# A decode block that streams its cache: other buffers for the last head's values, wo and w2

## The chip, the core and the metric

The kernel runs on one core of one Trainium2 chip. The metric is the device time of one execution in microseconds, as the median of several runs. The profile shows one execution, and its own time is given beside its span.

## What is computed

One token passes through an attention block with a key and value cache and a gated feed-forward block. A sigmoid gate mixes the two results. All data are float32.

```python
# x (1,1,512), k_cache and v_cache (1,8,32768,128), wq (512,4096), wo (4096,512), w1, w3 (512,1792), w2 (1792,512)
g = _sigmoid((x * gate_w).sum(-1, keepdims=True))
q = (x @ wq).reshape(B, Sq, 32, 128).transpose(0, 2, 1, 3)
k, v = jnp.repeat(k_cache, 4, axis=1), jnp.repeat(v_cache, 4, axis=1)
p = _softmax(jnp.einsum("bhqd,bhkd->bhqk", q, k) * (128 ** -0.5), axis=-1)
a = jnp.einsum("bhqk,bhkd->bhqd", p, v).transpose(0, 2, 1, 3).reshape(B, Sq, 4096) @ wo
b = (_silu(x @ w1) * (x @ w3)) @ w2
return g * a + (1 - g) * b
```

## The kernel before

There are 8 key and value heads, each serving 4 query heads. The keys of one head are 16.8 MB and so are its values. They are loaded in two halves of 8.39 MB. On chip there are three regions of that size, 128 partitions by 16384 floats each: `ra` takes the first half of a head's keys, `rb` the second half, and `rc` one half of its values at a time. At the start `rc` holds wq, and `rb` holds w1 and w3.

All large loads are issued by SyncE (SP) on one DMA queue, in an order that is written out by hand, with a semaphore wait ahead of each load whose region must first come free. Two counters tell when that is so:

- `c_k` counts the scores products: `2*h + 1` means that the first half of head h's keys (in `ra`) has been used, `2*h + 2` that the second half (in `rb`) has been.
- `c_v` counts the values products in the same way: `2*h + 1` after the first half of head h's values, `2*h + 2` after the second.

VectorE (DVE) turns the keys in place in their region, in blocks of 32 by 32 (`turned`), and signals each piece with `t_tr`. TensorE (PE) runs a loop over the heads. A step makes the scores of the first half (`scores(0, ra)`), the sum of the previous head's probabilities (`norm`), the first half of the previous head's values (`values(0, rc)`), the scores of the second half (`scores(1, rb)`), the second half of the previous head's values (`values(1, rc)`), and then the small products that bring the scores into the form for the softmax (`flips`, `heads`, `maxima`). So the values of a head are used one step after its keys. ScalarE (ACT) moves the scores out of PSUM and takes the exponentials.

The last head's values have no step to follow them. After the loop PE runs `norm`, `values(0, rc)` and `values(1, rb)` for it. A few small steps then turn the 32 heads' outputs into the weights `oq` of the last products. The product with wo follows in 32 pieces, 16 for each half of wo, and then that with w2 in 14 pieces, loaded as 6, 4, 3 and 1 of them. The feed-forward hidden vector (`htp`) is ready since the start of the kernel. The result is copied out of PSUM and stored by SP, which ends the kernel.

In the last round of SP's order (`h = 7`), the kernel before loads the first half of the last values into `rc` after `c_v` 14, the second half into `rb` after `c_k` 16, wo into `ra` without a wait of its own, and w2 into `rc` after `c_v` 15.

Of the kernel before, what the change touches and what calls it, by code (L numbers as in the profile page):

```python
# [24 lines left out]
@with_exitstack  # L25
def kernel(ctx, tc, x, k_cache, v_cache, wq, wo, w1, w3, w2, gate_w, out):
    with tc.tile_critical():
        _program(tc.nc, x, k_cache, v_cache, wq, wo, w1, w3, w2, gate_w, out)


def _program(nc, x, k_cache, v_cache, wq, wo, w1, w3, w2, gate_w, out):
    pe, dve, act, pool, sp = nc.tensor, nc.vector, nc.scalar, nc.gpsimd, nc.sync
    _, HKV, S, DH = k_cache.shape
    D = x.shape[-1]
# [4 lines left out]
    FR = F // P  # L39
# [6 lines left out]
    def sb(name, *shape):  # L46
        return nc.alloc_sbuf_tensor(name, [P, *shape], F32).ap()

    def token(name):
        return nc.alloc_semaphore(name)  # L50

    def count(name):
        return Count(nc, name)


    ra, rb, rc = sb("ra", W), sb("rb", W), sb("rc", W)
# [9 lines left out]
    oq = sb("oq", 64)  # L66
# [14 lines left out]
    def bank(n, w=1):  # L81
# [6 lines left out]

    l_x, l_q, l_k0 = token("l_x"), token("l_q"), token("l_k0")
    l_a, l_b, l_c = count("l_a"), count("l_b"), token("l_c")  # L90
    l_w1, l_w3, l_v = token("l_w1"), token("l_w3"), token("l_v")
    l_wo = [token(f"l_wo{i}") for i in range(2)]
    l_w2 = [token(f"l_w2{i}") for i in range(4)]
    l_out = token("l_out")
# [1 line left out]
    c_q, c_k, c_v, c_f, c_m, c_n, c_h, c_e = (  # L96
        count(n) for n in ("c_q", "c_k", "c_v", "c_f", "c_m", "c_n", "c_h", "c_e")
    )
# [10 lines left out]
    kd = k_cache.rearrange("a h (p m n) d -> (a h) m p (n d)", p=P, m=2, n=NK)  # L109
    vd = v_cache.rearrange("a h (r p n) d -> (a h) r p (n d)", r=2, p=P, n=NK)  # L110
    half = W // 2
# [4 lines left out]
    l_a.by(sp.dma_start(ra[:, half:W], kd[0, 0][:, half:W]), 16)  # L116
    sp.wait_ge(c_e.sem, 2)
    l_b.by(sp.dma_start(rb, kd[0, 1]), 16)
    for h in range(HKV):

        if h < HKV - 1:
            sp.wait_ge(c_k.sem, 2 * h + 1)
            l_a.by(sp.dma_start(ra, kd[h + 1, 0]), 16)
        if h:
            sp.wait_ge(c_v.sem, 2 * h)
        else:
            sp.wait_ge(c_dve.sem, 1)
        sp.dma_start(rc, vd[h, 0]).then_inc(l_c, 16)
        sp.wait_ge(c_k.sem, 2 * h + 2)
        if h < HKV - 1:  # L130
            l_b.by(sp.dma_start(rb, kd[h + 1, 1]), 16)
            sp.wait_ge(c_v.sem, 2 * h + 1)
            sp.dma_start(rc, vd[h, 1]).then_inc(l_c, 16)
        else:
            sp.dma_start(rb, vd[h, 1]).then_inc(l_v, 16)
    wod = wo.rearrange("(p k) e -> p (k e)", k=32)
    for i in range(2):
        sp.dma_start(ra[:, i * half:(i + 1) * half], wod[:, i * half:(i + 1) * half]).then_inc(l_wo[i], 16)
    w2t = rc[:, 0:FR * D].rearrange("p (k e) -> p k e", e=D)
    w2d = w2.rearrange("(p k) e -> p k e", k=FR)  # L140
    W2 = (0, 6, 10, 13, 14)
    sp.wait_ge(c_v.sem, 2 * HKV - 1)
# [33 lines left out]
    for c in range(NC):  # L176
        for b in range(2):
            for j in range(4):
# [3 lines left out]
                    start=(c == 0), stop=(c == NC - 1),  # L182
# [72 lines left out]
    def values(r, region):  # L255
        for g in range(4):
            for f in range(2):
                for t in range(4):
                    w = 512 * r + 64 * (2 * g + f) + 16 * t
                    n = 64 * f + 16 * g + 4 * t  # L260
                    i = pe.matmul(  # L261
                        o_ps[32 * t:32 * t + 32, :], prob[:, w:w + 32], region[:, n * DH:(n + 4) * DH],
                        start=(r == 0 and g == 0 and f == 0), stop=(r == 1 and g == 3 and f == 1),
                    )
        i.then_inc(c_v.sem, 1)
# [26 lines left out]
    def norm():  # L292
        take(t_p, REP)
        pe.matmul(mc[:, 0:REP], ones, sums, start=True, stop=True).then_inc(c_n.sem, 1)
# [32 lines left out]
    def inverted(h):  # L327
        dve.wait_ge(c_n.sem, h + 1)
        local.by(dve.reciprocal(recip, mc[:, 0:REP]))
        return local.n  # L330
# [40 lines left out]


    norm()
    pe.wait_ge(l_c, 16)
    values(0, rc)
    n_inv = inverted(HKV - 1)
    pe.wait_ge(l_v, 16)
    values(1, rb)
    act.wait_ge(c_v.sem, 2 * HKV)
    act.copy(ob, o_ps).then_inc(t_ob, 1)  # L380
# [15 lines left out]
    acc, pb = s_ps[1], s_ps[0]  # L396
    take(t_e)
    for k in range(32):
        if k % 16 == 0:
            pe.wait_ge(l_wo[k // 16], 16)  # L400
        t = k % 4
        pe.matmul(  # L402
            acc[32 * t:32 * t + 32, :], oq[:, k:k + 32], ra[:, k * D:(k + 1) * D], start=(k < 4), stop=False,
            skip_group_check=True,
        )
    pe.wait_ge(l_w2[0], 16)
    for k in range(W2[1]):
        t = k % 4
        i = pe.matmul(
            acc[32 * t:32 * t + 32, :], htp[:, k, :], w2t[:, k, :], start=False, stop=(k >= W2[1] - 4),  # L410
            skip_group_check=True,
        )
# [52 lines left out]
```

## Time and profile before

| | |
|---|---|
| time, median of 3 runs | 706.71 us (705.87 to 709.12) |
| time of the profiled execution | 706.43 us |
| its span, first to last instruction | 704.4 us |
| read from HBM | 296.23 MB, 421 GB/s over the span |
| mean granted TensorE clock | 0.798 |

The span is shorter than the time by what lies around the first and the last instruction, 2.03 us here. In the profile a line number such as L128 is a line of the kernel. "SPq" is SP issuing a DMA, and the duration of such an entry is that of the issue, not of the transfer. How long the transfer took to land is in the DMA view, counted from the start of the issue. Matmuls in float32 appear as two instructions each, so 32 products are listed as x64.

### The profile page before, as it was taken

How to read it: one execution, taken by the hardware profiler on the slowest of the kernel's cores; microseconds unless marked ns; L12 is line 12 of the kernel's file. 1: busy time of each engine (PE TensorE's matmuls, PEld its weight loads, DVE VectorE, ACT ScalarE, POOL GpSimd, SP SyncE). 2: the span in 40 equal slices, each digit the busy share in tenths (PEclk: the TensorE clock that was granted, in tenths of full speed). 3: DMA queues.
4: the chain of work that ended last, by engine and by line, in shares of the span. 5: the costliest groups of instructions: out<-in, count | busy, mean ns of one | idle time of the engine just before them, and what ended most of it. 6: DMA issues, size and time to landing. Idle time of an engine off the chain costs nothing. (4 is left out here: it accounts for less than half of the span.)

```text
span 704.4 us, 6586 instructions
## 1 busy us (share of the span) xinstructions
PE 364.7 (52%) x2944; PEld 101.5 (14%) x2944; DVE 308.1 (44%) x208; ACT 37.4 (5%) x93; POOL 7.1 (1%) x41
## 2 busy tenths in 40 slices
PE   0546255565554837264735746373716554470475
PEld 0110010113010301012110301021101301030121
DVE  0049469181907354362809172544618190730000
ACT  0000011001000010001000200001000100001000
POOL 0000000000000000000000000000000000000000
PEclk9987698788786979587777869696867888695779
DMA  9999999999999999999999999999999999939996
GB/s 410 402 434 422 467 414 428 428 450 424 428 450 428 424 432 450 421 432 440 439 424 424 454 424 432 428 443 432 424 454 424 425 435 443 424 141 466 417 418 273
DMA packets 6353, 296.35 MB, mean 421 GB/s; under 512 B 964, under 2 KB 968, under 8 KB 1224
## 3 DMA queue, kind: packets, MB, share of 16 engines
q1 hardware_dynamic: 6056, 296.23, 97.5%
q8 instruction: 6, 0.10, 0.1%
q10 hardware_dynamic: 288, 0.00, 0.0%
q14 instruction: 3, 0.02, 0.0%
HBM read 296.23 MB, written 0.00 MB: 421 GB/s over the span
## 5 line engine op out<-in xcount | busy, mean ns | idle before, releaser
L319 DVE STREAM_TRANSPOSE rb<-rb 128x2048 f32<-128x2048 f32 x64 | 141.8, 2275 | 151.8 <-DMA rb<-in_A_k_cache_dram 151.8
L248 PE MATMUL psum<-rb,winbuf 128*32 128x512 f32 x512 | 91.1, 790 | 148.1 <-PEq L106 148.1
L319 DVE STREAM_TRANSPOSE ra<-ra 128x2048 f32<-128x2048 f32 x64 | 141.4, 2275 | 45.4 <-DMA ra<-in_A_k_cache_dram 45.4
L248 PE MATMUL psum<-ra,winbuf 128*32 128x512 f32 x512 | 91.8, 795 | 111.3 <-PEq L106 111.3
L261 PE MATMUL psum<-rc,prob 128*32 128x512 f32 x960 | 111.4, 617 | 17.1 <-DMA rc<-in_A_v_cache_dram 15.0
L261 PEld LDWEIGHTS psum<-rc,prob 128*32 128x32 f32 x960 | 33.7, 114 | 89.8 <-issue 74.7
L354 DVE TENSOR_REDUCE mx<-psum 128x4 f32<-128x1024 f32 x8 | 9.8, 1225 | 82.9 <-PE psum L271 82.9
L248 PEld LDWEIGHTS psum<-rb,winbuf 128*32 128x32 f32 x512 | 13.2, 121 | 222.6 <-issue 222.6
L248 PEld LDWEIGHTS psum<-ra,winbuf 128*32 128x32 f32 x512 | 13.2, 121 | 180.6 <-issue 180.6
L334 ACT COPY sbuf<-psum 128x512 f32<-128x512 f32 x16 | 9.9, 621 | 481.1 <-PE psum L248 481.1
L323 DVE SCALAR_TENSOR_TENSOR otall<-psum,gate,recip 128x4 f32<-128x4 f32 x8 | 1.7, 213 | 45.2 <-PE psum L281 45.2
L366 ACT ACTIVATE prob<-psum,nm 128x256 f32<-128x256 f32 x32 | 18.9, 696 | 34.6 <-DVE nm L363 34.6
L271 PE MATMUL psum<-ident,sbuf 128*64 128x64 f32 x512 | 16.7, 223 | 0.8 <-PEq L106 0.8
L271 PEld LDWEIGHTS psum<-ident,sbuf 128*64 128x64 f32 x512 | 15.6, 138 | 8.2 <-issue 8.2
L261 PE MATMUL psum<-rb,prob 128*32 128x512 f32 x64 | 9.1, 731 | 10.8 <-DMA rb<-in_A_v_cache_dram 10.8
L174 PE MATMUL psum<-gsm,ones 128*128 128x1 f32 x2 | 0.6, 346 | 25.7 <-PEq L106 25.7
L235 POOL COPY winbuf<-winraw 32x16 f32<-32x16 f32 x32 | 6.1, 190 | 538.0 <-PE psum L248 498.3
L167 DVE COPY xp<-xs 128x4 f32<-128x4 f32 x1 | 0.2, 172 | 22.9 <-DMA gw<-in_gate_w_dram 22.9
L180 PE MATMUL psum<-rc,xp 128*32 128x512 f32 x64 | 9.5, 762 | 0.0
L207 PE MATMUL psum<-rb,xp 128*32 128x448 f32 x64 | 8.0, 653 | 2.8 <-DMA rb<-in_B_w_dram 2.8
L402 PE MATMUL psum<-ra,oq 128*32 128x512 f32 x64 | 7.3, 595 | 4.0 <-DMA ra<-in_A_wo_dram 3.6
L281 PE MATMUL psum<-fold,ob 128*128 128x4 f32 x64 | 8.4, 255 | 0.8 <-PEq L106 0.8
(56 smaller groups left out, 71.5 us busy)
## 6 DMA issues: line engine op xcount, KB each, us to landing
ra<-in_A_k_cache_dram SPq DMA_DIRECT2D x2, 4096.0 KB, 53.3
ra<-in_A_wo_dram SPq DMA_DIRECT2D x2, 4096.0 KB, 56.0
rb<-in_B_w_dram SPq DMA_DIRECT2D x2, 3584.0 KB, 34.9
rc<-in_B_w_dram SPq DMA_DIRECT2D x1, 1536.0 KB, 34.1
rc<-in_B_w_dram SPq DMA_DIRECT2D x1, 1024.0 KB, 36.3
rc<-in_B_w_dram SPq DMA_DIRECT2D x1, 768.0 KB, 37.6
rc<-in_B_w_dram SPq DMA_DIRECT2D x1, 256.0 KB, 37.8
rc<-in_A_v_cache_dram SPq DMA_DIRECT2D x15, 31.2
```

The costliest lines, as they stand in the source:

```text
L180: m = pe.matmul(pq[b][32 * j:32 * j + 32, :], xp[:, c, :], rc[:, o:o + REP * DH], start=(c == 0), stop=(c == NC - 1),)
L207: i = pe.matmul(ps[32 * j:32 * j + 32, 0:FJ], xp[:, c, :], rb[:, o:o + FJ], start=(c == 0), stop=(c == NC - 1))
L235: pool.tensor_copy(winbuf[32 * r:32 * r + 32, 16:144].rearrange("p (c k) -> p c k", k=32)[:, :, 4 * r:4 * r + REP], winraw[32 * r:32 * r + ...
L248: i = pe.matmul(s_ps[m][32 * g:32 * g + 32, :], winbuf[:, w:w + 32], region.rearrange("p (n c i) -> p c n i", c=4, i=32)[:, c, n:n + 16], ...
L261: i = pe.matmul(o_ps[32 * t:32 * t + 32, :], prob[:, w:w + 32], region[:, n * DH:(n + 4) * DH], start=(r == 0 and g == 0 and f == 0), stop ...
L271: i = pe.matmul(pf[64 * s:64 * s + 64, 64 * a:64 * a + 64], sbuf[:, a].rearrange("p i m -> p (i m)"), ident.rearrange("p (gf r s q) -> p s ...
L281: i = pe.matmul(mb[:, 0:REP], ob[:, b * P:(b + 1) * P], fold[:, 4 * b:4 * b + 4], start=(b == 0), stop=(b == 3))
L319: dve.transpose(part[:, c], part[:, c]).then_inc(t_tr, 1)
L334: act.copy(sbuf[:, :, :, m], s_ps[m].rearrange("p (n i) -> p n i", i=32)).then_inc(t_ev, 1)
L354: dve.tensor_reduce(mx, pf.rearrange("p (a q) -> p q a", q=REP), axis=AX.X, op=ALU.max).then_inc(t_mx, 1)
L366: act.activation(prob[:, 0:1024].rearrange("p (a n q) -> p n a q", a=16, q=REP)[:, :, :, q], pf.rearrange("p (n a q) -> p n a q", n=16, q= ...
L402: pe.matmul(acc[32 * t:32 * t + 32, :], oq[:, k:k + 32], ra[:, k * D:(k + 1) * D], start=(k < 4), stop=False, skip_group_check=True,)
```

## The change

SP's loop ends one head earlier, and the last round is written out behind it. The first half of the last head's values goes to `ra` after `c_k` 15, and the second half to `rb` after `c_k` 16 as before. wo goes to `rc` after `c_v` 14, and w2 to `ra` after `c_v` 15. Each half of the last values has a semaphore of its own (`l_v[0]`, `l_v[1]`). PE reads the regions accordingly. What is loaded and computed is the same, and so is the order of the loads.

```diff
-    l_w1, l_w3, l_v = token("l_w1"), token("l_w3"), token("l_v")
+    l_w1, l_w3 = token("l_w1"), token("l_w3")
+    l_v = [token(f"l_v{i}") for i in range(2)]
...
-    for h in range(HKV):
-
-        if h < HKV - 1:
-            sp.wait_ge(c_k.sem, 2 * h + 1)
-            l_a.by(sp.dma_start(ra, kd[h + 1, 0]), 16)
+    for h in range(HKV - 1):
+
+        sp.wait_ge(c_k.sem, 2 * h + 1)
+        l_a.by(sp.dma_start(ra, kd[h + 1, 0]), 16)
         if h:
             sp.wait_ge(c_v.sem, 2 * h)
         else:
             sp.wait_ge(c_dve.sem, 1)
         sp.dma_start(rc, vd[h, 0]).then_inc(l_c, 16)
         sp.wait_ge(c_k.sem, 2 * h + 2)
-        if h < HKV - 1:
-            l_b.by(sp.dma_start(rb, kd[h + 1, 1]), 16)
-            sp.wait_ge(c_v.sem, 2 * h + 1)
-            sp.dma_start(rc, vd[h, 1]).then_inc(l_c, 16)
-        else:
-            sp.dma_start(rb, vd[h, 1]).then_inc(l_v, 16)
+        l_b.by(sp.dma_start(rb, kd[h + 1, 1]), 16)
+        sp.wait_ge(c_v.sem, 2 * h + 1)
+        sp.dma_start(rc, vd[h, 1]).then_inc(l_c, 16)
+
+    sp.wait_ge(c_k.sem, 2 * HKV - 1)
+    sp.dma_start(ra, vd[HKV - 1, 0]).then_inc(l_v[0], 16)
+    sp.wait_ge(c_k.sem, 2 * HKV)
+    sp.dma_start(rb, vd[HKV - 1, 1]).then_inc(l_v[1], 16)
     wod = wo.rearrange("(p k) e -> p (k e)", k=32)
+    sp.wait_ge(c_v.sem, 2 * HKV - 2)
     for i in range(2):
-        sp.dma_start(ra[:, i * half:(i + 1) * half], wod[:, i * half:(i + 1) * half]).then_inc(l_wo[i], 16)
-    w2t = rc[:, 0:FR * D].rearrange("p (k e) -> p k e", e=D)
+        sp.dma_start(rc[:, i * half:(i + 1) * half], wod[:, i * half:(i + 1) * half]).then_inc(l_wo[i], 16)
+    w2t = ra[:, 0:FR * D].rearrange("p (k e) -> p k e", e=D)
...
-    pe.wait_ge(l_c, 16)
-    values(0, rc)
+    pe.wait_ge(l_v[0], 16)
+    values(0, ra)
     n_inv = inverted(HKV - 1)
-    pe.wait_ge(l_v, 16)
+    pe.wait_ge(l_v[1], 16)
     values(1, rb)
...
-            acc[32 * t:32 * t + 32, :], oq[:, k:k + 32], ra[:, k * D:(k + 1) * D], start=(k < 4), stop=False,
+            acc[32 * t:32 * t + 32, :], oq[:, k:k + 32], rc[:, k * D:(k + 1) * D], start=(k < 4), stop=False,
```

## The prediction

> **What bounds the kernel now.** I read the page first: the busy shares, then the forty slices.
>
> ```profile
> PE 364.7 (52%) x2944; PEld 101.5 (14%) x2944; DVE 308.1 (44%) x208; ACT 37.4 (5%) x93; POOL 7.1 (1%) x41
> ...
> DMA  9999999999999999999999999999999999939996
> GB/s 410 402 434 422 467 414 428 428 450 424 428 450 428 424 432 450 421 432 440 439 424 424 454 424 432 428 443 432 424 454 424 425 435 443 424 141 466 417 418 273
> ```
>
> No engine is above 52%, while the DMA digit is 9 in every slice but slice 35 (counting from 0) and the last. The kernel streams its 296 MB at one rate, and its time is that of the stream plus the places where nothing moves. A slice is 704.4/40 = 17.6 us, so the hole at 141 GB/s lies between 616.4 and 634.0 us. The change rewrites the queue just there.
>
> Second, the chain that ended last, which says whether that hole is paid for:
>
> ```profile
> 622.74 7.11 PE psum L261 x64
> ...
> 629.86 22.98 DMA rc<-in_A_v_cache_dram
> ...
> 652.89 8.59 PE psum L261 x64
> ...
> 662.35 37.63 DMA rc<-in_B_w_dram
> ...
> 700.03 1.12 PE psum L419 x32
> ```
>
> From the hole to the end it runs through transfers: the second values product of head 6 (7.11 us), then the first half of head 7's values, and at the end the last piece of w2, which lands at 662.35 + 37.63 = 699.98; 1.12 us of PE work and the store follow. The end of the kernel is the end of the stream plus 704.4 - 700.0 = 4.4 us.
>
> Third, the DMA queue in order of time: start of each issue, its length, and what is loaded (three stretches of the timeline of SP).
>
> ```profile
> 552.85 0.33 SPq L128 DMA_DIRECT2D rc<-in_A_v_cache_dram  x1
> 553.22 0.43 SPq L131 DMA_DIRECT2D rb<-in_A_k_cache_dram  x1
> ...
> 591.16 0.33 SPq L133 DMA_DIRECT2D rc<-in_A_v_cache_dram  x1
> 629.86 0.33 SPq L128 DMA_DIRECT2D rc<-in_A_v_cache_dram  x1
> 630.23 0.43 SPq L135 DMA_DIRECT2D rb<-in_A_v_cache_dram  x1
> 630.71 1.01 SPq L138 DMA_DIRECT2D ra<-in_A_wo_dram  x2
> 661.50 1.80 SPq L144 DMA_DIRECT2D rc<-in_B_w_dram  x4
> ```
>
> Fourth, the DMA view for the stretches around three of these issues: the last number is us from issue to landing.
>
> ```profile
> rc<-in_A_v_cache_dram SPq DMA_DIRECT2D x1, 31.1
> rb<-in_A_k_cache_dram SPq DMA_DIRECT2D x1, 50.0
> ```
> ```profile
> rc<-in_A_v_cache_dram SPq DMA_DIRECT2D x1, 31.4
> ```
> ```profile
> rc<-in_A_v_cache_dram SPq DMA_DIRECT2D x1, 23.0
> rb<-in_A_v_cache_dram SPq DMA_DIRECT2D x1, 42.0
> ```
>
> The landings, each issue plus its time: head 7's second keys 553.22 + 50.0 = 603.2; head 6's second values (I write v61; v70 and v71 are the two halves of head 7's) 591.16 + 31.4 = 622.6; v70 629.86 + 23.0 = 652.9; v71 630.23 + 42.0 = 672.2. From the keys to v61 it is 19.4, from v70 to v71 again 19.4: that is what 8.39 MB (128 x 16384 x 4 bytes) take behind another transfer. From v61 to v70 it is 30.3. So the hole is 30.3 - 19.4 = 10.9 us: 629.86 - 622.6 = 7.3 us in which nothing was queued, and 23.0 - 19.4 = 3.6 us in which the stream starts again. It exists because v70 goes into rc, and rc is free only when PE has multiplied by v61, which itself has just landed.
>
> **The change, part by part.** What the moved waits mean is read from when PE reaches them.
>
> ```profile
> 582.38 1.07 PE L248 MATMUL psum<-ra,winbuf 128*32 128x512 f32 x8 [1.13 <-PEq L106]
> 584.04 7.07 PE L261 MATMUL psum<-rc,prob 128*32 128x512 f32 x64 [0.28 <-PEq L106]
> 621.16 1.06 PE L248 MATMUL psum<-rb,winbuf 128*32 128x512 f32 x8 [1.13 <-PEq L106]
> 637.32 0.56 PE L294 MATMUL psum<-sums,ones 128*128 128x4 f32 x2 [2.74 <-PEq L106]
> ```
>
> v70 goes to ra and waits for the 15th scores product, over at 582.38 + 1.07 = 583.5. SP stands before it in the wait for the 13th values product, over at 584.04 + 7.07 = 591.1, and has then issued v61. So v70 follows v61 at about 591.5 instead of 629.86, and stands behind it in the queue 31 us before v61 lands. The wait is passed at once; the hole's 7.3 us and, since the stream never stops, its 3.6 us of restart go.
>
> The 3.6 us are the less certain part: the trace shows a transfer behind another (19.4) and one into an empty queue (23.0), and the new v70 is of the first kind, like v71, so I take all of it. If a restart stayed, the gain would be 7.3. The Trainium skill ("DMA: Bandwidth & Descriptors", section "Latency and other measured facts") puts the fixed cost of a DMA at about 2 us; by it the gain would be 7.3 + 2 = 9.3 us, and the profiled time 697.1. The row here is 1.6 us above that figure.
>
> v71 still goes to rb after the 16th scores product, at 621.16 + 1.06 = 622.2, now with only v70 ahead of it: issued at 622.3 instead of 630.23. v70 will land at 622.6 + 19.4 = 642.0, so this issue has 19.7 us of cover, less 3.6 for a start. wo and w2 stand behind that wait on SP; both come later anyway.
>
> wo goes to rc and gets a wait of its own, for the 14th values product: 622.74 + 7.11 = 629.85, then 1.0 us for its two issues. v71 lands at 642.0 + 19.4 = 661.4; cover 31 us. Before, the same issue was made at 630.71, so this wait costs nothing.
>
> w2 goes to ra after the 15th values product. That needs v70 (642.0) and head 7's probabilities; the sum behind them is done at 637.32 + 0.56 = 637.9, so the landing comes last, by 4 us. The product takes 8.59 us: w2 is issued at 642.0 + 8.6 = 650.6 instead of 661.50. It must be there before wo has landed, at 661.4 + 19.7 = 681.1 (19.7 is worked out with the rows below), less 3.6: cover 27 us.
>
> PE's own work is the same: the same number of products, on other regions, and a second counter in place of a wait that was there. I cost that at nothing; it hides behind the stream as the next rows show.
>
> ```profile
> 672.26 9.09 PE L261 MATMUL psum<-rb,prob 128*32 128x512 f32 x64 [10.84 <-DMA rb<-in_A_v_cache_dram]
> 684.74 3.64 PE L402 MATMUL psum<-ra,oq 128*32 128x512 f32 x32 [0.38 <-PEq L106]
> 692.00 3.64 PE L402 MATMUL psum<-ra,oq 128*32 128x512 f32 x32 [3.62 <-DMA ra<-in_A_wo_dram]
> 695.69 1.91 PE L409 MATMUL psum<-rc,htp 128*32 128x512 f32 x12
> 698.17 1.08 PE L419 MATMUL psum<-rc,htp 128*32 128x128 f32 x32 [0.57 <-DMA rc<-in_B_w_dram]
> ```
>
> After v71 (672.26) come the product, the small steps to 684.74, the first half of wo, and then a wait of 3.62 us for its second half, which lands at 692.0, 19.7 us after v71; w2 ends 8.0 us later. In the changed kernel v71, wo and w2 follow each other at the same distances, only 10.9 us earlier, so this tail moves as a block: v71 661.4, second half of wo 681.1, w2 689.1, end of the span 689.1 + 4.4 = 693.5.
>
> **Sum.** The profiled execution took 706.43 us around its span of 704.4; 706.43 - 10.9 = 695.5 us. It stands 0.28 below the median of 706.71 (runs 705.87 to 709.12), so I leave it there.
>
> **Rivals.** *The tail turns from stream to PE.* The cover in the tail is 3.62 us, and PE does not always have its full clock (columns: stretch, its length, busy times, then clock, DMA share and rate):
>
> ```profile
> 635.00:656.00 21.00, 3.67 (x18) 1.29 (x22) 0.18 (x1) 2.17 (x8) 0.00 (x0) 0.51 1.01 435
> 656.00:666.00 10.00, 5.42 (x52) 1.32 (x44) 0.00 (x0) 0.00 (x0) 0.00 (x0) 1.00 1.03 446
> 666.00:676.00 10.00, 3.74 (x20) 0.99 (x24) 0.00 (x0) 0.00 (x0) 0.00 (x0) 0.51 0.86 370
> 676.00:704.00 28.00, 18.33 (x206) 6.72 (x198) 0.99 (x4) 1.17 (x2) 0.00 (x0) 0.99 0.80 339
> ```
>
> Were the clock at half from wo's second half on, its 3.64, 1.91, 1.08 and 1.12 us would double to 15.5 us, and PE would end at 681.1 + 15.5 = 696.6 instead of 700.03 + 1.12 - 10.9 = 690.3: 6.3 us more, 701.8. For it speaks that half clock is granted over 20 us at a stretch; against it that both half stretches begin while PE waits and end some 3 to 4 us into a product (652.89 to 656, 672.26 to 676), and the tail keeps its wait of 10.8 us before v71 and its dense work behind. The Trainium skill ("TensorE: Matmul & The Clock Gate", section "Part 1: The HAM clock gate") has it that an idle array falls to half clock and about 3.4 us of work lift it; by that rule the tail comes out as before. The trace agrees, with the two delays just given.
>
> *The stream is slower without its pause.* Behind v61 there are 3 x 8.39 + 3.67 = 28.8 MB, which take 689.1 - 622.6 = 66.5 us here, 433 GB/s. At the lowest full slice, 402, they take 71.7: 700.7 us in all. But v70 to v71, with wo queued behind, shows the usual 19.4.
>
> *The change doesn't fill the hole.* If something other than the missing issue stopped the stream, the time stays 706.4. Against it: between 591.5 and 629.86 SP issues nothing.
>
> *Slower: the queue shares instead of serving in turn.* The new thing is that v61, which PE needs first, has 8.39 MB beside it at once, with head 7's keys still 11.7 us short. If the three shared the stream, the keys would land at 591.5 + 3 x 11.7 = 626.6, the 16th scores product end 19.0 later, at 645.6, while v61 and v70 (7.7 left of each) landed at 642.0: a new hole to 649.2. v71, issued at 645.6, would then share with wo's halves (from 653.2) and w2 (from about 670), and land last of all with them: 649.2 + 19.4 + 19.7 + 8.0 = 696.3. Behind v71 PE still has 9.1 (its product), 3.4 (to 684.74), 7.3 (wo), 1.9 and 2.2 (w2) = 23.9 us: it ends at 720.2 instead of 701.15, 19.1 later, 725.5 in all. It turns to a loss where v71 lands later than 701.15 - 23.9 = 677. Against it: v and k, issued 0.37 us apart at 553, landed 31.1 and 50.0 later, one after the other, with another transfer ahead of them.
>
> **How the numbers follow.** About 0.5%, 3.5 us, is what can be told from no change here. Forecast: 87%. PE tail at half clock: 5% (701.8, still faster). Slower stream: 3% (700.7, faster). No effect: 2%. Sharing: 3%. So faster 0.95, same 0.02, slower 0.03. The range ends above where the restart stays, 695.5 + 3.6 = 699.1, and below at twice the runs' spread under the median (2 x 0.84), 693.8. The cases beyond it hold 13%.
>
> **What would show it.** In the changed kernel's profile slice 35 moves over 400 GB/s. v70 is issued within a microsecond of v61 and lands some 19.4 us after it, at about 642; v71 at 661, second half of wo at 681, w2's last piece at 689. SP has no long wait ahead of v70; the chain's end is again w2's last piece and 4.4 us. The prediction is wrong if v61 lands later than 623, if PE waits for nothing ahead of wo's second half, if the rate after 622 lies below 420, or if the span is above 697.

## The result, and the profile after

The changed kernel takes 695.02 us (median of 6 runs, 694.79 to 695.14) against 706.86 us (6 runs, 705.87 to 709.12): a ratio of 0.983, 95% interval 0.9815 to 0.9845. Run again with the experiments it took 695.28 us (5 runs, 694.68 to 697.25) against 706.96 (0.9834, 0.9809 to 0.986). The profiled execution took 694.79 us with a span of 692.7; the forecast was 695.5 us.

The forty slices of the changed kernel (the DMA engines' busy tenths, and what they moved):

```profile
span 692.7 us, 6586 instructions
...
DMA  9999999999999999999999999999999999999996
GB/s 390 413 438 452 421 432 428 447 443 428 424 431 428 443 447 428 428 431 428 439 443 435 428 428 431 431 443 439 431 424 431 431 443 443 428 424 431 432 419 279
```

No digit but the last is under 9, and slices 35 and 36, which cover 606 to 641 us, have 424 and 431 GB/s where slice 35 before had 141. SP's issues in the changed kernel, then the time from issue to landing of the two values transfers issued at 591 (v61, v70) and of the one at 622 (v71):

```profile
590.91 0.33 SPq L132 DMA_DIRECT2D rc<-in_A_v_cache_dram  x1
591.28 0.43 SPq L135 DMA_DIRECT2D ra<-in_A_v_cache_dram  x1
622.52 0.33 SPq L137 DMA_DIRECT2D rb<-in_A_v_cache_dram  x1
630.28 0.80 SPq L141 DMA_DIRECT2D rc<-in_A_wo_dram  x2
650.13 1.75 SPq L147 DMA_DIRECT2D ra<-in_B_w_dram  x4
```
```profile
rc<-in_A_v_cache_dram SPq DMA_DIRECT2D x1, 31.1
ra<-in_A_v_cache_dram SPq DMA_DIRECT2D x1, 50.1
```
```profile
rb<-in_A_v_cache_dram SPq DMA_DIRECT2D x1, 38.2
```

v61 lands at 590.91 + 31.1 = 622.0, v70 at 591.28 + 50.1 = 641.4 and v71 at 622.52 + 38.2 = 660.7: distances of 19.4 and 19.3 us, where v61 to v70 was 30.3. v70 is issued 0.37 us behind v61 instead of 38.7, and v61 still takes its 31 us. The end of the chain that ended last:

```profile
641.44 8.67 PE psum L264 x64
...
650.97 37.32 DMA ra<-in_B_w_dram
...
688.34 1.12 PE psum L422 x32
```

It is the old end: the piece of w2 that the chain names lands at 650.97 + 37.32 = 688.3 instead of 699.98, and 4.4 us follow. In both kernels this is the third of the four pieces (768 KB); the small fourth lands some 0.6 us later.

### The profile page after: what moved, and what is told of

The parts are those of the page before. It is cut to its first block, busy times and chain, and to the rows that moved or that the text cites. A ratio compares the mean times of both kernels' runs of the same rounds, so it can differ in the third digit from the quotient of the medians.

```text
span 692.7 us, 6586 instructions
## 1 busy us (share of the span) xinstructions
PE 367.9 (53%) x2944; PEld 101.3 (15%) x2944; DVE 308.1 (44%) x208; ACT 37.4 (5%) x93; POOL 7.1 (1%) x41
## 5 line engine op out<-in xcount | busy, mean ns | idle before, releaser
L251 PE MATMUL psum<-ra,winbuf 128*32 128x512 f32 x512 | 94.1, 815 | 110.5 <-PEq L107 110.5
L264 PE MATMUL psum<-rc,prob 128*32 128x512 f32 x896 | 102.9, 612 | 2.1 <-PEq L107 2.1
L264 PEld LDWEIGHTS psum<-rc,prob 128*32 128x32 f32 x896 | 31.5, 113 | 69.4 <-issue 69.3
L264 PE MATMUL psum<-ra,prob 128*32 128x512 f32 x64 | 8.6, 698 | 3.2 <-DMA ra<-in_A_v_cache_dram 3.2
L405 PE MATMUL psum<-rc,oq 128*32 128x512 f32 x64 | 7.3, 595 | 3.7 <-DMA rc<-in_A_wo_dram 3.3
## 6 DMA issues: line engine op xcount, KB each, us to landing
ra<-in_B_w_dram SPq DMA_DIRECT2D x1, 1536.0 KB, 33.8
ra<-in_B_w_dram SPq DMA_DIRECT2D x1, 768.0 KB, 37.3
```

The lines of the kernel that those rows point to most:

```text
L251: i = pe.matmul(s_ps[m][32 * g:32 * g + 32, :], winbuf[:, w:w + 32], region.rearrange("p (n c i) -> p c n i", c=4, i=32)[:, c, n:n + 16], ...
L264: i = pe.matmul(o_ps[32 * t:32 * t + 32, :], prob[:, w:w + 32], region[:, n * DH:(n + 4) * DH], start=(r == 0 and g == 0 and f == 0), stop ...
L405: pe.matmul(acc[32 * t:32 * t + 32, :], oq[:, k:k + 32], rc[:, k * D:(k + 1) * D], start=(k < 4), stop=False, skip_group_check=True,)
```

## The experiments

By the theory that stood after the result, the time of v70's issue is all that matters, and the 11 us are 7.3 us of empty queue and some 3.6 us of starting it again. Its rivals were that the regions themselves matter, that a start costs less, and that the waits moved further down the queue cost or gain something of their own.

**The regions without the earlier issue.** v70 goes to `ra`, but waits as before.

```diff
-    sp.wait_ge(c_k.sem, 2 * HKV - 1)
+    sp.wait_ge(c_v.sem, 2 * HKV - 2)
     sp.dma_start(ra, vd[HKV - 1, 0]).then_inc(l_v[0], 16)
```

> The changed kernel with its regions, but v70 waits for the 14th values product, as in the kernel before. Theory (only the time of v70's issue matters, not the region): the hole is back, v70 issued at about 630 and landed 23 us later, 706.4 to 706.9 us. Rival (the regions themselves, or the free rc, make the stream faster): at or near 695 us, or anything clearly between.

Measured: 706.8 us (11 runs, 705.7 to 709.4) against 706.01 us for the kernel before in the same set of runs; ratio 1.0009 (0.9996 to 1.0023). SP's issue of v70, and its time to landing:

```profile
630.33 0.33 SPq L135 DMA_DIRECT2D ra<-in_A_v_cache_dram  x1
```
```profile
ra<-in_A_v_cache_dram SPq DMA_DIRECT2D x1, 22.9
```

v70 lands at 653.2, as late as in the kernel before (652.9), and the hole stands in slice 35 again at 126 GB/s. The regions are worth nothing by themselves; they only allow the earlier issue.

**A start without idle time.** v70 waits for the 16th scores product, which ends just as v61 lands.

```diff
-    sp.wait_ge(c_k.sem, 2 * HKV - 1)
+    sp.wait_ge(c_k.sem, 2 * HKV)
     sp.dma_start(ra, vd[HKV - 1, 0]).then_inc(l_v[0], 16)
```

> The changed kernel with one wait moved: the first half of the last values (v70) goes to ra only after the 16th scores product, as the second half does, not after the 15th. It is then issued at about 622.3 us, within half a microsecond of the landing of head 6's second values (v61, 622.0): no idle queue, but a start into an empty one. Theory (the 10.9 us are 7.3 without work and 3.6 of restart): v70 lands 23.0 us after its issue, at 645.3 instead of 641.4, so 695.0 + 3.9 = 698.9 us. By the fixed cost of about 2 us that the Trainium skill states (DMA: Bandwidth & Descriptors, Latency and other measured facts) it would be 622.3 + 19.4 + 2.0 = 643.7, that is 697.3 us. Rival (a start costs nothing, only the idle time counts): 695.4 us at most.

Measured: 699.24 us (698.37 to 699.52), ratio 0.9908 (0.9893 to 0.9923). SP's issues in this kernel, and its three values transfers' times to landing:

```profile
592.22 0.33 SPq L132 DMA_DIRECT2D rc<-in_A_v_cache_dram  x1
622.09 0.33 SPq L135 DMA_DIRECT2D ra<-in_A_v_cache_dram  x1
622.47 0.43 SPq L137 DMA_DIRECT2D rb<-in_A_v_cache_dram  x1
```
```profile
rc<-in_A_v_cache_dram SPq DMA_DIRECT2D x1, 30.2
```
```profile
ra<-in_A_v_cache_dram SPq DMA_DIRECT2D x1, 22.9
rb<-in_A_v_cache_dram SPq DMA_DIRECT2D x1, 41.9
```

v70 is issued at 622.09, 0.3 us before v61 has landed (592.22 + 30.2 = 622.4), and lands at 645.0: 22.6 us after v61 instead of 19.4. So 3.2 us go although the queue is never without work by SP's book. The forecast of this run, 698.9, holds; 697.3 and 695.4 lie below every run. In the same set of runs the changed kernel with w2 issued later, which lost nothing (below), took 695.26 us, 10.8 less than the kernel before (706.01). Of these this one keeps 6.8 (706.01 - 699.24), about the idle time. The other 4.0 need the transfer queued well ahead of the end of the one before it.

Not all of the 4.0 us is the start: v61 itself lands some 0.4 us later here, and in the profiled execution (698.37, the shortest of the four) the end of the chain is not w2 but PE, whose products with the second half of wo are slow (3.64 us in the changed kernel):

```profile
683.92 5.34 PE psum L405 x32
```

What the three longer runs added was not profiled.

**The same start at another place.** w2 is issued only when wo has landed.

```diff
     sp.wait_ge(c_v.sem, 2 * HKV - 1)
+    sp.wait_ge(l_wo[1], 16)
     for i in range(4):
```

> The changed kernel, with w2 issued only when the second half of wo has landed (about 680.3 us instead of 650.1): the queue runs empty once more, with no time lost before the next issue. Theory (a start into an empty queue costs 3.6 us): w2 ends 3.6 to 3.9 us later, 698.6 to 698.9 us. By a fixed cost of about 2 us as the Trainium skill states it (DMA: Bandwidth & Descriptors, Latency and other measured facts): 697.0 to 697.3 us. Rival (w2's 34 to 37 us from issue to landing are a latency that has to be covered): 680.3 + 37 + 4.4 = 721.7 for the span, 723.8 us.

Measured: 698.05 us (697.86 to 699.61), ratio 0.9897 (0.9881 to 0.9912): 3.0 us over the changed kernel's 695.02. SP's issue of w2, the four pieces' times to landing, and the stretches around it (length, busy times, clock, DMA share, GB/s), first here and then in the changed kernel:

```profile
680.75 1.83 SPq L148 DMA_DIRECT2D ra<-in_B_w_dram  x4
```
```profile
ra<-in_B_w_dram SPq DMA_DIRECT2D x1, 1536.0 KB, 6.2
ra<-in_B_w_dram SPq DMA_DIRECT2D x1, 1024.0 KB, 8.3
ra<-in_B_w_dram SPq DMA_DIRECT2D x1, 768.0 KB, 9.7
ra<-in_B_w_dram SPq DMA_DIRECT2D x1, 256.0 KB, 9.9
```
```profile
676.00:678.00 2.00, 2.00 (x16) 0.57 (x12) 0.00 (x0) 0.00 (x0) 0.00 (x0) 0.64 0.76 328
678.00:680.00 2.00, 1.74 (x19) 0.28 (x8) 0.00 (x0) 0.00 (x0) 0.00 (x0) 1.00 0.23 98
680.00:682.00 2.00, 1.29 (x12) 0.42 (x16) 0.00 (x0) 0.00 (x0) 0.00 (x0) 1.00 0.30 74
682.00:684.00 2.00, 2.00 (x24) 0.52 (x16) 0.00 (x0) 0.00 (x0) 0.00 (x0) 1.00 0.83 301
```
```profile
676.00:678.00 2.00, 1.00 (x12) 0.09 (x4) 0.00 (x0) 0.00 (x0) 0.00 (x0) 1.00 0.85 365
678.00:680.00 2.00, 0.00 (x0) 0.00 (x0) 0.00 (x0) 0.00 (x0) 0.00 (x0) 1.00 0.97 412
680.00:682.00 2.00, 1.71 (x16) 0.55 (x20) 0.00 (x0) 0.00 (x0) 0.00 (x0) 1.00 1.00 422
682.00:684.00 2.00, 1.96 (x24) 0.42 (x17) 0.00 (x0) 0.00 (x0) 0.00 (x0) 1.00 0.99 412
```

The rival that needs 37 us of warning for w2 falls: the first piece lands 6.2 us after its issue, at 686.95, where the changed kernel has it at 650.13 + 33.8 = 683.9. The size of the start was missed: 3.0 us by the medians, where 3.6 to 3.9 were expected, and 2.0 to 2.3 by the fixed cost cited in the expectation. Between the two landings it is 2.6: the second half of wo is used from 680.71 instead of 680.29, so 0.4 of the 3.0 us lie ahead of its landing. The windows show where such a start is paid. They count a packet, the unit in which a transfer moves, whole in the row in which it starts, so their edges are blurred, but the two kernels can be compared row by row. With w2 held back the stream is thin before wo has landed (0.76 and 0.23 of the DMA engines' time, against 0.85 and 0.97) and after w2 is issued (0.30 and 0.83, against 1.00 and 0.99). We read the first part as engines that are done with wo early and have nothing to go on with.

**The cover of w2's issue.**

```diff
-    sp.wait_ge(c_v.sem, 2 * HKV - 1)
+    sp.wait_ge(c_v.sem, 2 * HKV)
     for i in range(4):
```

> The changed kernel, with w2 issued after the 16th values product (about 670.0 us) instead of the 15th (650.1). The prediction gave the issue of w2 a cover of 27 us up to 677.5. Theory: 20 of the 27 us are used and nothing changes, 695.0 us; w2 still lands at 688.3, so 18 us after its issue instead of 37. Rival (the landing follows the issue at a fixed distance): 670.0 + 37.5 + 4.4 = 711.9 for the span, 713.9 us.

Measured: 695.26 us (694.73 to 697.57), ratio 0.9861 (0.9846 to 0.9876). The chain that ended last in this kernel:

```profile
670.88 17.40 DMA ra<-in_B_w_dram
...
688.32 1.12 PE psum L422 x32
```

w2 is issued 20 us later and the same piece of it lands at 688.28 as before, 17.4 us after its issue instead of 37.3. At least these 20 of the 27 us of cover are there, and the 20 us by which the time to landing shrank were time in the queue.

**How much room PE has in the tail.** 32 more products stand between the halves of wo.

```diff
     for k in range(32):
+        if k == 16:
+            for e in range(32):
+                t = e % 4
+                pe.matmul(
+                    mc[32 * t:32 * t + 32, :], oq[:, e % 16:e % 16 + 32], rc[:, (e % 16) * D:(e % 16 + 1) * D],
+                    start=(e < 4), stop=(e >= 28), skip_group_check=True,
+                )
         if k % 16 == 0:
```

> The changed kernel with 32 more products on PE between the two halves of wo (into a spare PSUM bank, their result is not used): 32 x 0.2275 = 7.3 us at full clock, where PE waits 3.3 us for the second half of wo and 0.6 and 0.6 us for pieces of w2. Theory (the tail is covered by the stream up to that wait, no further): 7.3 - 3.3 - 1.2 = 2.8 us more, 697.8 us; with half clock in part of it some us more. Rival (the stream alone sets the end, PE has much more room): 695.0 us. Rival (PE is on the path already): 702.3 us.

Measured: 697.88 us (696.0 to 700.67), ratio 0.9872 (0.9843 to 0.9902). The median is where it was expected, but that is chance: the runs fall into two groups, three at 696.0 to 696.4 and three at 699.4 to 700.7, and none lies within 1.4 us of it. In the profiled one (696.38) the added products took 7.08 us at full clock and the span grew by 1.6 us, so the room there is about 5.5 us rather than the 4.5 of the three waits. PE has some room, but not much more: in this execution the chain that ended last is PE alone from 673.3 us on. What the upper group met wasn't profiled.

**A busy PE ahead of the tail.** 40 products more fill its wait for v71.

```diff
+    for e in range(40):
+        t = e % 4
+        pe.matmul(
+            s_ps[0][32 * t:32 * t + 32, :], winbuf[:, 0:32], flat[:, 512:1024], start=(e < 4), stop=(e >= 36),
+            skip_group_check=True,
+        )
     pe.wait_ge(l_v[1], 16)
     values(1, rb)
```

> The changed kernel with 40 products more on PE while it waits for the second half of the last values (into a spare PSUM bank, not used): PE then doesn't idle for 10.7 us ahead of the tail, and the product behind it, 9.2 us in the changed kernel, should run at full clock in 7.1. Theory (the clock in the tail is covered by the stream): the time stays at 695.0 us. Rival (the tail hangs on the clock): up to 2 us less, 693.0 us.

Measured: 694.95 us (694.83 to 696.92), ratio 0.983 (0.9805 to 0.9855): no change, as by the theory. Products of the tail in this kernel:

```profile
660.90 7.08 PE L264 MATMUL psum<-rb,prob 128*32 128x512 f32 x64 [1.87 <-DMA rb<-in_A_v_cache_dram]
671.35 5.34 PE L411 MATMUL psum<-rc,oq 128*32 128x512 f32 x32 [0.38 <-PEq L107]
680.32 6.55 PE L411 MATMUL psum<-rc,oq 128*32 128x512 f32 x32 [3.63 <-DMA rc<-in_A_wo_dram]
```

The product behind v71 runs in 7.08 us as expected, but the products with wo then take 5.34 and 6.55 us instead of 3.64 each. That execution took 696.02 us, 1.1 over the median. So the run shows that 2.1 us saved behind v71 gain nothing; a tail at full clock throughout it doesn't show.

**Filling the hole with wo.** The order behind v61 becomes wo, v70, v71, w2; wo goes to `ra`, v70 and later w2 to `rc`.

```diff
+    wod = wo.rearrange("(p k) e -> p (k e)", k=32)
     sp.wait_ge(c_k.sem, 2 * HKV - 1)
-    sp.dma_start(ra, vd[HKV - 1, 0]).then_inc(l_v[0], 16)
+    for i in range(2):
+        sp.dma_start(ra[:, i * half:(i + 1) * half], wod[:, i * half:(i + 1) * half]).then_inc(l_wo[i], 16)
+    sp.wait_ge(c_v.sem, 2 * HKV - 2)
+    sp.dma_start(rc, vd[HKV - 1, 0]).then_inc(l_v[0], 16)
     sp.wait_ge(c_k.sem, 2 * HKV)
     sp.dma_start(rb, vd[HKV - 1, 1]).then_inc(l_v[1], 16)
...
```

> Another order in the hole: behind head 6's second values come wo into ra (after the 15th scores product), then the first half of the last values into rc (after the 14th values product), the second half into rb, and w2 into rc. The queue never runs empty here either. If the stream alone sets the time: 695.0 us. Theory (the stream sets the end only while PE's work behind the last values stays covered): the last half of the values lands at 622.3 + 3 x 19.5 = 680.8 instead of 660.8, and PE still has 9.2 + 3.4 + 7.3 + 1.9 + 2.2 = 24.0 us behind it: its end at 704.8, and 3.3 us to the end of the span and 2.0 around it, 710.1 us, about 4 us slower than before the change, without any hole.

Measured: 712.52 us (12 runs, 708.71 to 715.52), ratio 1.0072 (1.0052 to 1.0092): slower than the kernel before. Its slices and the chain that ended last (the profiled execution took 709.59 us):

```profile
DMA  9999999999999999999999999999999999999980
...
693.42 7.07 PE psum L405 x64
700.49 0.98 PE psum L412 x9
```

There is no hole, the stream is over before the last slice of 17.7 us, and the end of the chain is PE alone. The last half of the values lands at 680.9, and PE's work behind it, 23.4 us, ends at 704.3. The median lies 2.4 us above the forecast; the profiled execution is one of the shortest, and what the longer runs added was not profiled. A full queue gains nothing where what it brings last has the longest work behind it.

## Why the prediction was right

*The hole.* The step from landings, 30.3 - 19.4 = 10.9 us, is what the chip gave back: the same two landings are 19.4 us apart in the changed kernel, and putting the late issue back alone brings the old time back (ratio 1.0009). Of the 11.6 us between the two profiled executions 10.9 are this. Another 0.5 us lie before any moved instruction: v61 lands at 622.0 instead of 622.6. In the variants of the changed kernel above it lands between 622.1 and 622.6, so this half microsecond may be chance. The rest, 0.2 us, is within the rounding of these rows; the runs can't tell it.

*Its two terms.* 7.3 us of empty queue and 3.6 us of restart were added. The run that keeps only a start lost 3.2 us between the landings and 4.0 us by the medians; the second place lost 2.6 and 3.0. For v70 the row was nearer than the 2 us that the Trainium skill ("DMA: Bandwidth & Descriptors", section "Latency and other measured facts") states; for w2 the 2.6 us between the landings lie nearer to the 2 us than to 3.6. And "restart" names only a part of the term. These are rows of the kernel before around the hole (the stretch, its length, busy times, clock, DMA share, GB/s):

```profile
619.00:620.00 1.00, 1.00 (x8) 0.12 (x8) 1.00 (x1) 0.00 (x0) 0.00 (x0) 1.00 0.46 197
620.00:621.00 1.00, 0.03 (x3) 0.00 (x0) 1.00 (x1) 0.00 (x0) 0.00 (x0) 1.00 0.00 0
...
629.00:630.00 1.00, 1.00 (x16) 0.26 (x10) 0.00 (x0) 0.13 (x1) 0.00 (x0) 1.00 0.00 0
630.00:631.00 1.00, 1.00 (x42) 1.00 (x38) 0.00 (x0) 0.45 (x1) 0.00 (x0) 1.00 1.81 590
```

No packet starts between 620 and 630 us, although v61 lands only at 622.6. So a part of the 3.6 us is lost ahead of that landing, and not behind v70's issue.

*The covers.* v71, wo and w2 were forecast to be issued 16 to 31 us ahead of need at no cost. They were issued at 622.52, 630.28 and 650.13 (forecast 622.3, 630 and 650.6), and 20 us less for w2 changed nothing.

*The tail.* It moved as a block: v71 660.7, second half of wo about 680.3, w2 688.3, against 661.4, 681.1 and 689.1. The difference is the 0.5 us from before v61 and a little more. What the prediction called w2's last piece is the third of four; as the fourth comes 0.6 us behind it in both kernels, the sum doesn't change. PE's wait ahead of the second half of wo is 3.30 us, where it was 3.62:

```profile
680.29 3.64 PE L405 MATMUL psum<-rc,oq 128*32 128x512 f32 x32 [3.30 <-DMA rc<-in_A_wo_dram]
```

*The rivals.* Sharing is refuted: v61's 31.1 us are unchanged with v70 behind it. The slower stream is too: 424 to 432 GB/s in slices 35 to 37, and the 28.8 MB behind v61 take 688.3 - 622.0 = 66.3 us where 66.5 were forecast. The rival of the half clock was mis-sized in two ways. Its 5% stood for a half clock that sets the time, but the clock itself falls in the tail much more often: in five of the ten profiled executions of this document 16 products with wo took 4.9 us or more instead of 3.64 (in one of them the row has both halves together, 9.94 us). One of the five is another execution of the changed kernel (the products, then the stretch, its length, busy times, clock, DMA share, GB/s):

```profile
673.92 9.94 PE L405 MATMUL psum<-rc,oq 128*32 128x512 f32 x64 [0.38 <-PEq L107]
```
```profile
672.00:680.00 8.00, 6.82 (x36) 2.16 (x35) 0.70 (x3) 0.00 (x0) 0.00 (x0) 0.57 0.98 419
680.00:690.00 10.00, 8.15 (x120) 3.14 (x116) 0.29 (x1) 0.58 (x1) 0.00 (x0) 1.00 0.73 302
```

But its price was never 6.3 us here: this execution took 694.68 us, the least of its set, because the half clock was over by 680 us and the cover took it up: the products with wo ended at 683.86, where they end at 683.93 with the wait of 3.30 us. PE waited for nothing ahead of wo's second half there, which the prediction had named as a sign that it is wrong; it is none. In the profiled execution with 40 products more, where it reached the second half of wo, the time is 1.1 us over the median. The prediction's sentence that the tail "comes out as before" was wrong for the products of these executions, and right only for the time.

## What to carry to other kernels

Where one stream bounds a kernel, look for the slice in which it stops, take the distance of two landings less that of two in the flow, and ask which region's release the queue was waiting for; a region that is already free at that moment is worth the whole distance. Queue the next transfer well ahead of the end of the last, not at it: a start at the very end still cost about 3 us here. And before the order of loads is changed for that, add up the work behind each one's landing: wo in the same hole kept the stream full and made the kernel slower.

## What the runs showed of the hardware that was not expected

An empty queue is paid for on both sides: with w2 held back, the engines' share had fallen to 0.23 in the window of 2 us that ends 0.7 us before wo's landing was reported, and was back at 0.83 only in the window from 682 us, after w2's issue at 680.75.

In the one execution profiled, keeping PE busy with 40 products ahead of the tail didn't hold its clock through the tail: the products with wo, 12 and 21 us later, took 5.34 and 6.55 us against 3.64. Where the tail hangs on PE, the time scatters more: 708.71 to 715.52 us with wo in the hole, 694.68 to 697.25 in the eleven runs of the changed kernel. That the clock makes this scatter is not shown. The mean granted clock of a whole run doesn't order the times (0.792 for 708.71, 0.791 for 715.03), and it can't tell what the tail had.
